# A linear-attention and adapter kernel: Q turned raw with relu on the way out of PSUM, sine taken from cosine by a tangent, all casts done by the loads, and a new written-out order

## The chip, the cores and the metric

The kernel runs on one core of a Trainium2 chip. The metric is device time in microseconds (us) of one execution. A core has engines that each work through their own instruction list in order: TensorE (PE in the profile, with PEld for its weight loads), VectorE (DVE), ScalarE (ACT), GpSimd (POOL) and SyncE (SP). [...] Transfers between HBM and the on-chip memory SBUF are issued by SyncE or GpSimd and carried by 16 DMA engines. TensorE writes to PSUM, from which VectorE and ScalarE move results to SBUF.

## The reference

Inputs are q, k and v of 8 batches, 8 heads, 576 positions and 64 features in float32, and small router weights. Cut to what matters:

```python
theta = pi/2 * pos / S                      # per position
phi(x) = concat([relu(x)*cos, relu(x)*sin]) # 128 features
kv  = einsum('bhsf,bhsd->bhfd', phi(k), v)
z   = phi(k).sum(over s)
x   = (phi(q) @ kv) / (phi(q) . z + 1e-6)   # attention output, (4608, 512)
logits = x @ w_gate                         # 8 experts
w = softmax of the two largest logits
out = x + sum over the two experts e of w_e * (x @ A[e]) @ B[e]   # rank 16
```

The output is 4608 by 512 in float32 (9.4 MB); q, k and v are 9.4 MB each.

## The kernel before, in words

**Tiling.** Positions are split as p*9 + j, with 64 values of p and 9 of j. The work goes in four pairs P of batches (2P and 2P+1). For each pair the kernel first builds the two feature matrices, then runs nine steps j of 128 rows (64 positions of each batch). Rows leave in units of three steps (the last pair has units of 3, 3, 2 and 1).

**Building a pair.** V arrives by GpSimd's loads, which cast float32 to bf16 (`ld_vh`, `ld_full`). `vscale` (L374) writes V times cos and V times sin into VV; since the weights depend on the position only, scaling V serves instead of scaling K. For pairs 1 to 3 the sine half is a GpSimd product of two tensors and the cosine half a VectorE product. K of the first pair comes as float32 by SyncE (`ld_f`) and ScalarE casts it with relu (L357); later K is cast by the load and gets relu on VectorE (L363). `kv_mm` (L388) multiplies K by VV on TensorE into pND, and `kv_evac` (L406, L408) copies it into BD, one half on ScalarE and one on VectorE. A column of cos and sin in VV yields z along with kv.

**Q.** All of q comes as float32 by SyncE into the eight F buffers. ScalarE casts it with relu into Qr (L368). In each step `qt_mm` (L469) turns Qr on TensorE, 128 columns at a time, into the PSUM tile pt, and `qt_evac` (L476) multiplies it by cos and by sin from the table TB in one VectorE product of 1024 elements, into qTcs.

**A step.** `num_mm` (L491) gives numerator and denominator in pND; VectorE takes the reciprocal (L504) and the product xt (L510). TensorE turns xt (L520) and ScalarE copies it (L526). For a unit, `za_mm` (L533) gives adapter inputs and logits in pza, VectorE and ScalarE do the two-expert softmax (`r_max`, `r_mask`, `r_sig`, L544 to L568), VectorE scales the adapter inputs (L571), TensorE turns them (L580), ScalarE copies (L585), `dx_mm` (L590, L591) adds x and the adapters' output in pdx, ScalarE copies to osb (L596) and SyncE stores (L602).

**What sets the order.** A planner in the file (`Planner.run`) lists all steps with their durations, due times, needs and buffers, plays them through once as the program is built, and emits the instructions in the order found, with a manual schedule. So each engine has one fixed list. Buffers come from pools of fixed size; a step that wants a buffer waits until its last user is done. PSUM has two pND tiles (two banks each), two pt, one pza and one pdx.

Of the kernel before, what the change touches and what calls it, by code (L numbers as in the profile page):

```python
# [19 lines left out]
LATENCY = {"PE": 0.25, "DVE": 0.12, "ACT": 0.15, "POOL": 0.2, "SP": 0.0}  # L20
DMA_GBPS = 0.400
DMA_LATENCY = 2.0
DMA_LANES = 8


class Step:
    __slots__ = ("eng", "dur", "emit", "needs", "makes", "uses", "due", "name",
                 "size", "preds", "start", "end", "seen", "idx")

    def __init__(self, eng, dur, emit, needs, makes, uses, due, name, size):  # L30
        self.eng, self.dur, self.emit = eng, dur, emit
        self.needs, self.makes, self.uses = needs, makes, uses
        self.due, self.name, self.size = due, name, size
        self.preds = []
        self.start = None


class Planner:
# [3 lines left out]
    def __init__(self):  # L42
        self.steps = []
        self.pools = {}
        self.slot = {}
        self.queue = {}
# [5 lines left out]
    def add(self, eng, dur, emit, due, needs=(), makes=(), uses=(), name="", size=0):  # L52
        s = Step(eng, dur, emit, list(needs), list(makes), list(uses), due, name, size)
        s.idx = len(self.steps)
        self.steps.append(s)
        return s

    def run(self):
# [5 lines left out]
        users = {}  # L64
        for s in self.steps:
            s.preds = [made[n] for n in s.needs]
            for u in s.uses:
                if u not in users and self.queue[u[0]] is not None:
                    self.queue[u[0]].append(u)
                users.setdefault(u, []).append(s)  # L70
        left = {u: len(v) for u, v in users.items()}
        free_at = {p: [0.0] * n for p, n in self.pools.items()}
        succ = [[] for _ in self.steps]
        npred = [0] * len(self.steps)
        for s in self.steps:
            for p in {id(p): p for p in s.preds}.values():
                succ[p.idx].append(s)
                npred[s.idx] += 1
        ready = {e: [] for e in LATENCY}
        for s in self.steps:  # L80
            if npred[s.idx] == 0:
                ready[s.eng].append(s)
        etime = {e: 0.0 for e in LATENCY}
        lanes = {"SP": [], "POOL": []}
        server = 0.0
        order = []
        while len(order) < len(self.steps):
            best = None
            for e, lst in ready.items():
                cands = []  # L90
                for s in lst:
# [4 lines left out]
                    for u in s.uses:  # L96
                        if u not in self.slot:
                            f = free_at[u[0]]
                            m = min(f)
                            fifo = self.queue[u[0]]  # L100
                            if m == math.inf or (fifo and fifo[0] != u):
                                ok = False
                                break
                            t = max(t, m)
# [8 lines left out]
                t, s = min((c for c in cands if c[0] <= m + 0.12), key=lambda c: (c[1].due, c[0]))  # L113
                if best is None or t < best[0]:
                    best = (t, s)
            if best is None:
                held = {u: self.slot[u] for u in self.slot if left[u]}
                raise RuntimeError(f"plan: no step can go: {[(s.name, s.makes[:1], [u for u in s.uses if u not in self.slot]) for v in ready.values() for s in v]} held {held}")
# [11 lines left out]
            s.seen = s.end + LATENCY[s.eng]  # L130
            if s.size:
                server = max(server, s.start + 0.6) + s.size / DMA_GBPS * 1e-6
                s.seen = server + DMA_LATENCY - 0.6
                lanes[s.eng].append(s.seen)
            etime[s.eng] = s.end
            for u in s.uses:
                left[u] -= 1
                if left[u] == 0:
                    free_at[u[0]][self.slot[u]] = max(x.seen for x in users[u])
# [13 lines left out]
def kernel(  # L153
# [23 lines left out]
    HALF_B = 128 * 2 * J * D * 4  # L177

# [3 lines left out]
    def sb(shape, dtype, name, n=None):  # L182
        if n is None:
# [4 lines left out]
    POOLS = {"F": 8, "V": 4, "K": 4, "Q": 4, "VV": 4, "BD": 4, "QT": 3, "XT": 12, "XTT": 6,  # L188
             "ZG": 2, "ZGT": 2, "OSB": 3, "M8": 2, "W": 2, "RD": 3,
             "pND": 2, "pT": 2, "pZA": 1, "pDX": 1}  # L190
# [9 lines left out]
    TBi = sb([128, J, NP], I32, "TBi")  # L200
    TB = sb([128, 2, J, NP], FP16, "TB")
# [6 lines left out]
    tF = sb([128, 2, J, D], FP32, "F", POOLS["F"])  # L208
    tV = sb([128, 4, J, D], BF16, "Vb", POOLS["V"])
    tK = sb([128, 4, J, D], BF16, "Kr", POOLS["K"])  # L210
    tQ = sb([128, 2, J, 2, D], BF16, "Qr", POOLS["Q"])
# [9 lines left out]
    tNA = sb([128, 3], FP32, "nasum", POOLS["M8"])  # L221
    tSG = sb([128, 3, E], FP32, "sig", POOLS["W"])
# [3 lines left out]
    pT = [psum.tile([128, 1024], BF16, name=f"pt{i}") for i in range(2)]  # L226
    pZA = psum.tile([128, 512], FP32, name="pza")
    pDX = psum.tile([128, 512], FP32, name="pdx")

    def S_(u):  # L230
        return pl.slot[u]

# [10 lines left out]
    def c_tbi():  # L243
        nc.gpsimd.iota(TBi, pattern=[[1, J], [J, NP]], base=0, channel_multiplier=0)

# [4 lines left out]
    def c_tb():  # L250
        nc.scalar.activation(TB[:, 1], TBi, AF.Sin, bias=0.0, scale=sc)
        nc.scalar.activation(TB[:, 0], TBi, AF.Sin, bias=halfpi[:, :], scale=-sc)

# [25 lines left out]
    pl.add("DVE", 0.1, c_halfpi, -50, makes=["halfpi"])  # L279
    pl.add("POOL", 0.5, c_tvi, -49.5, makes=["TVi"])  # L280
    pl.add("POOL", 0.9, c_tbi, -48.9, makes=["TBi"])
    pl.add("ACT", 2.0, c_tvf, -49, needs=["halfpi", "TVi"], makes=["TVf"])
    pl.add("ACT", 1.4, c_tb, -48, needs=["TBi", "TVf"], makes=["TB"])
    pl.add("ACT", 1.4, c_sig, -47, needs=["TB"], makes=["sigtab"])
    pl.add("DVE", 1.3, c_tv, -48, needs=["TVf"], makes=["TV"])
    for i in range(4):
        pl.add("DVE", 0.15, c_vcol(i), -47 + i, needs=["TVf"], makes=[("vcol", i)])
        pl.add("DVE", 0.4, c_bd(i), -40 + i, makes=[("bd", i)])
    pl.add("POOL", 1.0, c_ident, -47, makes=["ident"])
    pl.add("POOL", 3.0, c_s4, -20, needs=["ident"], makes=["S4"])  # L290
# [11 lines left out]
    pl.add("POOL", 0.9, w_a, -9, makes=["Ald"], size=1024 * 512)  # L302
    pl.add("POOL", 0.3, w_g, -9, makes=["Gld"], size=128 * 512)
    pl.add("POOL", 0.3, w_b, -8, makes=["Ball"], size=128 * 2048)

    def w_turn():
        for c in range(4):
            for i in range(4):
                nc.tensor.matmul(out=pDX[:, c * 128:(c + 1) * 128], lhsT=S4[:, i, c * 128:(c + 1) * 128],
                                 rhs=Ald[:, :, i, :], start=(i == 0), stop=(i == 3))  # L310
        for c in range(4):
            for i in range(4):
                nc.tensor.matmul(out=pZA[:, c * 8:(c + 1) * 8], lhsT=S4[:, i, c * 128:(c + 1) * 128],
                                 rhs=Gld[:, i, :], start=(i == 0), stop=(i == 3))

    def w_aw():
        nc.scalar.copy(AW[:, :, 0:ER], pDX.rearrange("p (c x) -> p c x", c=4))
        nc.scalar.copy(AW[:, :, ER:AW_W], pZA[:, 0:32].rearrange("p (c x) -> p c x", c=4))

    pl.add("PE", 2.0, w_turn, 2, needs=["S4", "Ald", "Gld"], makes=["AWp"],  # L320
           uses=[("pDX", "w"), ("pZA", "w")])
    pl.add("ACT", 0.8, w_aw, 3, needs=["AWp"], makes=["AW"], uses=[("pDX", "w"), ("pZA", "w")])


    T = 2.35
# [14 lines left out]
    def ld_f(x, b, a, u):  # L340
        def f():
            nc.sync.dma_start(out=flat(tF[S_(u)]), in_=half_src(x, b, a))
        return f

    def ld_vh(b, a, u):
        def f():
            nc.gpsimd.dma_start(out=flat(tV[S_(u)])[:, 2 * a:2 * a + 2], in_=half_src(v, b, a))  # L347
        return f

    def ld_full(x, b, u, ts):  # L350
        def f():
            nc.gpsimd.dma_start(out=flat(ts[S_(u)]), in_=full_src(x, b))
        return f

    def relu_k_half(b, a, uf, uk):
        def f():
            nc.scalar.activation(tK[S_(uk)][:, 2 * a:2 * a + 2], tF[S_(uf)], AF.Relu)  # L357
        return f

    def relu_k_full(uk):  # L360
        def f():
            t = tK[S_(uk)].rearrange("p c j d -> p (c j d)")
            nc.vector.tensor_scalar(out=t, in0=t, scalar1=0.0, scalar2=None, op0=ALU.max)  # L363
        return f

    def relu_q(b, a, uf, uq):
        def f():
            nc.scalar.activation(tQ[S_(uq)][:, a].rearrange("p j h d -> p h j d"), tF[S_(uf)], AF.Relu)  # L368
        return f

    def vscale(eng, cs, lo, hi, uv, uvv):
        def f():
            n = hi - lo
            eng.tensor_tensor(  # L374
                out=tVV[S_(uvv)][:, lo:hi, :, cs * (D + 2):cs * (D + 2) + D],
                in0=tV[S_(uv)][:, lo:hi],
                in1=TV[:, cs].unsqueeze(1).to_broadcast([128, n, J, D]),
                op=ALU.mult)
# [18 lines left out]
    def kv_evac(par, aa, up, ubd, eng):  # L397
        def f():
            pt, bd = pND[S_(up)], tBD[S_(ubd)]
            lo, n = aa[0], len(aa)  # L400
            for hh in range(2):
                o = bd[64 * hh:64 * hh + 64, par, lo:lo + n, :, 66 * hh:66 * hh + W]
                i = pt[64 * hh:64 * hh + 64, par, lo * 2 * W:(lo + n) * 2 * W].rearrange(
                    "p (a c w) -> p a c w", a=n, c=2)
                if eng == "ACT":
                    nc.scalar.copy(o, i)  # L406
                else:
                    nc.vector.tensor_copy(o, i)  # L408
        return f

    for P in range(4):
        for a in range(2):
            for b2 in range(2):
                b = 2 * P + b2
                uk, uv, uvv, ubd, uq = ("K", b), ("V", b), ("VV", b), ("BD", b), ("Q", b)
                uf = ("F", "q", b, a)
# [283 lines left out]
```

## Time and profile before

| | |
|---|---|
| median time of 2 runs | 161.36 us (161.11 to 161.61) |
| span of the profiled execution | 159.0 us |
| granted TensorE clock, mean | 0.915 |
| HBM read, written | 28.85 MB, 9.44 MB |

The profile shows, for one execution, how long each engine was busy, in groups of instructions by line, engine and shapes. A row of a group gives the busy time and the mean time of one instruction in ns, then how long the engine had been idle before such instructions and what ended the wait. The timeline lists instructions by start and length. A wait is put down to what released it last. The chain of waits is the path followed back from the last instruction.

### The profile page before, as it was taken

The page shows a single profiled execution, that of the slowest core. Times are in us where ns is not written, and L with a number is a line of the kernel's source. Part 1 is how long each engine was busy: PE and PEld are TensorE (multiplying, and loading weights), DVE is VectorE, ACT ScalarE, POOL GpSimd, SP SyncE. Part 2 cuts the span into 40 slices and gives each one's busy share as a digit, 9 for nine tenths or more (in the row PEclk, how much of TensorE's full clock was granted, in tenths as well). Part 3 has the DMA queues.
Part 4 walks back from the last instruction along what each step waited for, and adds up shares of the span by engine and source line. Part 5 has one row for each costly group of instructions (what it writes and reads, how often), then busy time and mean ns, then how long its engine had stood idle before and what let it go on. Part 6 is the DMA issues. An engine that isn't in the chain of part 4 may idle for free.

```text
span 159.0 us, 4155 instructions
## 1 busy us (share of the span) xinstructions
PE 101.1 (64%) x1724; PEld 73.4 (46%) x1724; DVE 110.8 (70%) x273; ACT 84.2 (53%) x170; POOL 49.4 (31%) x39
## 2 busy tenths in 40 slices
PE   0014365237976977206957986889988888797650
PEld 0013244125954546103846864656656565465310
DVE  5335284886268466998999698987876787869510
ACT  4922943301666433800862467985686546664751
POOL 6995106813239206999950000000000000000000
PEclk9999999999998589955796599999999999999996
DMA  4999999999999999999910004004422440315044
GB/s 164 309 288 292 292 293 286 327 339 307 288 279 275 287 244 293 220 208 207 277 66 0 4 0 198 4 6 198 194 108 103 196 198 6 148 49 202 0 198 198
DMA packets 16081, 30.01 MB, mean 189 GB/s; under 512 B 1984, under 2 KB 9280, under 8 KB 16064
## 3 DMA queue, kind: packets, MB, share of 16 engines
q1 hardware_dynamic: 7312, 21.24, 36.2%
q0 software_dynamic: 8752, 8.53, 32.1%
q8 instruction: 13, 0.21, 0.5%
q14 instruction: 4, 0.03, 0.1%
HBM read 28.85 MB, written 9.44 MB: 241 GB/s over the span
## 4 chain that ended last, share of the span: by engine, by line
DVE 30%; PE 27%; DMA 21%; POOL 7%; ACT 7%; issue 5%; ACTq 0%; POOLq 0%
DMA Vb<-in_v_dram 21%; DVE VV L374 9%; PE pnd L491 6%; DVE xt L510 6%; DVE qTcs L476 5%; PE pdx L590 5%; PE pdx L591 4%; PE pnd L388 4%; PE pza L533 3%; DVE BD L408 3%; ACT osb L596 3%; DVE Kr L363 2%; PE pt L520 2%; POOL Vb L347 2%; DVE rden L504 2%
## 5 line engine op out<-in xcount | busy, mean ns | idle before, releaser
L491 PE MATMUL pnd<-BD,qTcs 128*64 128x130 bf16 x576 | 27.9, 243 | 17.6 <-DVE xt L510 8.3
L491 PEld LDWEIGHTS <-qTcs 128*64 128x64 bf16 x576 | 20.7, 120 | 25.4 <-issue 12.9
L374 POOL TENSOR_TENSOR VV<-Vb,TV 128x2304 bf16<-128x2304 bf16 x6 | 29.9, 4989 | 4.4 <-DMA Vb<-in_v_dram 4.2
L596 ACT COPY osb<-pdx 128x512 f32<-128x512 f32 x36 | 21.2, 588 | 16.4 <-PE pdx L591 16.2
L526 ACT COPY xT<-pt 128x512 bf16<-128x512 bf16 x36 | 21.1, 594 | 15.9 <-PE pt L520 15.7
L374 DVE TENSOR_TENSOR VV<-Vb,TV 128x1152 bf16<-128x1152 bf16 (+1 forms) x14 | 24.7, 1786 | 6.8 <-DMA Vb<-in_v_dram 6.7
L476 DVE TENSOR_TENSOR qTcs<-pt,TB 128x1024 bf16<-128x1024 bf16 (+1 forms) x45 | 25.0, 576 | 3.9 <-PE pt L469 3.6
L510 DVE TENSOR_TENSOR xt<-pnd,rden 128x512 bf16<-128x512 f32 (+1 forms) x45 | 26.3, 584 | 1.3
L388 PE MATMUL pnd<-VV,Kr 64*64 64x130 bf16 x576 | 14.1, 264 | 17.9 <-DVE VV L374 14.7
L368 ACT ACTIVATE Qr<-F 128x1152 bf16<-128x1152 f32 x16 | 18.5, 1169 | 6.2 <-DMA F<-in_q_dram 6.2
L388 PEld LDWEIGHTS <-Kr 64*64 64x64 bf16 x576 | 12.4, 135 | 19.3 <-issue 10.0
L469 PE MATMUL pt<-ident,Qr 128*128 128x128 bf16 x144 | 16.0, 242 | 7.4 <-ACT Qr L368 3.4
L590 PE MATMUL pdx<-xt,ident 128*128 128x512 bf16 x36 | 14.7, 408 | 4.0 <-ACT osb L596 3.9
L520 PE MATMUL pt<-ident,xt 128*128 128x128 bf16 x144 | 14.9, 232 | 3.1 <-DVE qTcs L476 1.1
L406 ACT CAST BD<-pnd 64x260 bf16<-64x260 f32 (+1 forms) x20 | 6.6, 332 | 18.7 <-PE pnd L388 12.7
L469 PEld LDWEIGHTS <-Qr 128*128 128x128 bf16 x144 | 10.5, 107 | 12.3 <-issue 5.6
L504 DVE RECIPROCAL rden<-pnd 128x8 f32<-128x8 f32 (+1 forms) x45 | 8.7, 192 | 10.5 <-PE pnd L491 10.4
L591 PE MATMUL pdx<-Ball,zgT 128*128 128x512 bf16 x36 | 14.5, 404 | 0.9 <-ACT zgT L585 0.8
L408 DVE CAST BD<-pnd 64x260 bf16<-64x260 f32 (+1 forms) x20 | 7.5, 374 | 9.4 <-ACT BD L406 7.2
L520 PEld LDWEIGHTS <-xt 128*128 128x128 bf16 x144 | 10.6, 103 | 7.4 <-issue 2.8
L533 PE MATMUL pza<-AW,xT 128*128 128x136 bf16 x144 | 12.2, 239 | 0.2 <-ACT xT L526 0.2
L561 ACT ACTIVATE sig<-pza,nasum 128x8 f32<-128x8 f32 x36 | 7.1, 269 | 8.0 <-DVE pza L551 8.0
(46 smaller groups left out, 92.2 us busy)
## 6 DMA issues: line engine op xcount, KB each, us to landing
F<-in_q_dram SPq DMA_DIRECT2D x16, 576.0 KB, 16.8
out_dram<-osb SPq DMA_DIRECT2D x11, 768.0 KB, 3.3
Vb<-in_v_dram POOLq DMA_DIRECT2D x6, 576.0 KB, 32.0
Kr<-in_k_dram POOLq DMA_DIRECT2D x6, 576.0 KB, 29.9
F<-in_k_dram SPq DMA_DIRECT2D x4, 576.0 KB, 9.0
Vb<-in_v_dram POOLq DMA_DIRECT2D x4, 288.0 KB, 10.5
out_dram<-osb SPq DMA_DIRECT2D x1, 512.0 KB, 2.6
out_dram<-osb SPq DMA_DIRECT2D x1, 256.0 KB, 2.0
```

What stands on the lines that cost most here:

```text
L368: nc.scalar.activation(tQ[S_(uq)][:, a].rearrange("p j h d -> p h j d"), tF[S_(uf)], AF.Relu)
L374: eng.tensor_tensor(out=tVV[S_(uvv)][:, lo:hi, :, cs * (D + 2):cs * (D + 2) + D], in0=tV[S_(uv)][:, lo:hi], in1=TV[:, cs].unsqueeze(1).to_ ...
L388: nc.tensor.matmul(out=pt[64 * hh:64 * hh + 64, par, a * 2 * W:(a + 1) * 2 * W], lhsT=kt[64 * par:64 * par + 64, 2 * a + hh, j, :], rhs=vt ...
L469: nc.tensor.transpose(out=pt[:, o:o + 128], in_=qt[:, a, j].rearrange("p h d -> p (h d)"), identity=ident)
L476: nc.vector.tensor_tensor(out=tQT[S_(uqt)][:, :, 0:n, :], in0=pT[S_(up)][:, 0:n * 64].rearrange("p (g s) -> p g s", g=n).unsqueeze(1).to_b ...
L491: nc.tensor.matmul(out=nd[64 * b2:64 * b2 + 64, a, 0:4 * W].rearrange("p (h e w) -> p h e w", h=2, e=2)[:, :, par], lhsT=qt[:, cs, (b2 * l ...
L510: nc.vector.tensor_tensor(out=tXT[S_(uxt)].rearrange("p (a h d) -> p a h d", a=2, h=4)[:, aa[0]:aa[-1] + 1], in0=nd_view(und, aa)[:, :, :, ...
L520: nc.tensor.transpose(out=pT[S_(up)][:, c * 128:(c + 1) * 128], in_=tXT[S_(uxt)][:, c * 128:(c + 1) * 128], identity=ident)
L526: nc.scalar.copy(tXTT[S_(uxtt)].rearrange("p c s -> p (c s)"), pT[S_(up)][:, 0:512])
L590: nc.tensor.matmul(out=pDX, lhsT=ident, rhs=tXT[S_(uxt)], start=True, stop=False)
L591: nc.tensor.matmul(out=pDX, lhsT=tZGT[S_(uzt)][:, i], rhs=Ball, start=False, stop=True)
L596: nc.scalar.copy(tOSB[S_(uo)][:, i], pDX)
```

## The change

It moves the casts, the relu and part of the scaling to other places, and writes the order anew.

- **Loads.** K, V and Q all come by GpSimd's casting loads straight to bf16 (`load`); the F buffers and ScalarE's cast of Q go, and SyncE issues stores only. The first pair comes in halves. K gets its relu in place, on VectorE, ScalarE or GpSimd (`relu_k`).
- **Q.** Raw Q is turned in 64-column pieces (two per former piece). ScalarE applies relu as it copies from PSUM, which gives relu(q) without the cosine. VectorE writes a second copy times tan. The cosine of the query row cancels between numerator and denominator, so cos and sin become 1 and tan. The tan table is built by two TensorE matmuls in place of two sine passes.
- **V.** GpSimd no longer runs a product of two tensors; where it scales V, it does so in nine one-input instructions with a per-partition scalar. ScalarE can do the same in nine activations, VectorE by the product with TV as before.
- **Router.** One sigmoid per unit, preceded by a small VectorE operation, in place of one per step.
- **PSUM.** pt, pza and pdx become one pool of four banks, ps. The evacuation of K times V is cut by heads instead of parity. qTcs has ten buffers instead of three, Q six instead of four.
- **Tail.** In the last pair's last two units the two matmuls of dx are separate steps, and osb is copied in two halves, one on each engine.
- **Order.** Each step has a due time from a table (PLACES), and, where there are alternatives, its engine from another (CHOICE). Of the twelve whole and eight half V products VectorE then has eight and five, ScalarE three and three, GpSimd one whole; ten of the xT, five of the zgT and six whole and two half osb copies go to VectorE.

```diff
+PLACES = [
...
+]
+CHOICE = [
...
+]
...
+        if PLACES is not None:
+            for s in self.steps:
+                s.due = PLACES[s.idx]
+                s.choose(CHOICE[s.idx])
...
-    POOLS = {"F": 8, "V": 4, "K": 4, "Q": 4, "VV": 4, "BD": 4, "QT": 3, "XT": 12, "XTT": 6,
+    POOLS = {"V": 4, "K": 4, "Q": 6, "VV": 4, "BD": 4, "QT": 10, "XT": 12, "XTT": 6,
              "ZG": 2, "ZGT": 2, "OSB": 3, "M8": 2, "W": 2, "RD": 3,
-             "pND": 2, "pT": 2, "pZA": 1, "pDX": 1}
+             "pND": 2, "pS": 4}
...
+    def c_tan_p():
+        nc.vector.memset(ones_f, 1.0)
+        nc.vector.reciprocal(tan_p, TVf[:, 0])
+        nc.vector.tensor_tensor(out=tan_p, in0=tan_p, in1=TVf[:, 1], op=ALU.mult)
...
+    def c_tan_mm():
+        d = tan_d.rearrange("p j s -> p (j s)")
+        nc.tensor.matmul(out=pF(("pS", "t0")), lhsT=ones_f, rhs=d[:, 0:512], start=True, stop=True)
+        nc.tensor.matmul(out=pF(("pS", "t1"))[:, 0:64], lhsT=ones_f, rhs=d[:, 512:576], start=True, stop=True)
...
-    def ld_f(x, b, a, u):
-        def f():
-            nc.sync.dma_start(out=flat(tF[S_(u)]), in_=half_src(x, b, a))
-        return f
...
-    def relu_q(b, a, uf, uq):
-        def f():
-            nc.scalar.activation(tQ[S_(uq)][:, a].rearrange("p j h d -> p h j d"), tF[S_(uf)], AF.Relu)
-        return f
...
+    def load(x, b, hs, ts, u):
+        def f():
+            if len(hs) == 4:
+                nc.gpsimd.dma_start(out=flat(ts[S_(u)]), in_=full_src(x, b))
...
+    def relu_k(eng, hs, uk):
+        def f():
+            t = tK[S_(uk)][:, hs[0]:hs[-1] + 1].rearrange("p c j d -> p (c j d)")
+            if eng == "ACT":
+                nc.scalar.activation(t, t, AF.Relu)
+            else:
+                (nc.gpsimd if eng == "POOL" else nc.vector).tensor_scalar(out=t, in0=t, scalar1=0.0, scalar2=None, op0=ALU.max)
...
+            if eng == "POOL":
+                for j in range(J):
+                    nc.gpsimd.tensor_scalar(out=o[:, :, j], in0=i[:, :, j], scalar1=TVf[:, cs, j:j + 1],
+                                            scalar2=None, op0=ALU.mult)
+            elif eng == "ACT":
+                for j in range(J):
+                    nc.scalar.activation(o[:, :, j], i[:, :, j], AF.Copy, scale=TVf[:, cs, j:j + 1])
...
     def qt_mm(P, j, aa, up):
...
-                    nc.tensor.transpose(out=pt[:, o:o + 128], in_=qt[:, a, j].rearrange("p h d -> p (h d)"),
-                                        identity=ident)
+                    for hh in range(2):
+                        nc.tensor.transpose(out=pt[64 * hh:64 * hh + 64, o:o + 128], in_=qt[:, 2 * a + hh, j, :],
+                                            identity=ident)
...
+    def qt_evac(aa, up, uqt):
+        def f():
+            n = 4 * len(aa)
+            nc.scalar.activation(tQT[S_(uqt)][:, 0, 0:n].rearrange("p g s -> p (g s)"), pB(up)[:, 0:n * 64], AF.Relu)
+        return f
+
+    def qt_tan(j, aa, uqt):
+        def f():
+            n = 4 * len(aa)
+            t = tQT[S_(uqt)]
+            nc.vector.tensor_tensor(out=t[:, 1, 0:n], in0=t[:, 0, 0:n],
+                                    in1=TT[:, j].unsqueeze(1).to_broadcast([128, n, NP]), op=ALU.mult)
+        return f
...
+            nc.vector.scalar_tensor_tensor(
+                out=tTT[S_(um)][:, 0:n], in0=lg, scalar=2.0,
+                in1=tNA[S_(um)][:, 0:n].unsqueeze(2).to_broadcast([128, n, E]), op0=ALU.mult, op1=ALU.add)
...
-            for i in range(n):
-                nc.scalar.activation(tSG[S_(uw)][:, i], za_v(n)[:, i, ER:AW_W], AF.Sigmoid,
-                                     bias=tNA[S_(um)][:, i:i + 1], scale=2.0)
+            nc.scalar.activation(tSG[S_(uw)][:, 0:n], tTT[S_(um)][:, 0:n], AF.Sigmoid)
```

## The prediction

> **What bounds the kernel now.** I read the page from the top: totals, then the slices, then the busy time of three stretches, then the chain and the timeline of the worst stretch.
>
> ```profile
> span 159.0 us, 4155 instructions
> PE 101.1 (64%) x1724; PEld 73.4 (46%) x1724; DVE 110.8 (70%) x273; ACT 84.2 (53%) x170; POOL 49.4 (31%) x39
> ...
> POOL 6995106813239206999950000000000000000000
> PEclk9999999999998589955796599999999999999996
> DMA  4999999999999999999910004004422440315044
> ```
>
> No engine is full over the span. A slice is 3.98 us: the DMA engines are full until about 80 us, then nearly idle. So the first half waits for loads and the second for computing. The stretches (columns: length, then busy us of PE, PEld, DVE, ACT, POOL, then the clock, DMA share and GB/s) say so in numbers:
>
> ```profile
> 0.00:46.00 46.00, 20.07 (x380) 15.90 (x380) 25.09 (x61) 20.37 (x32) 22.53 (x32) 1.00 1.08 290
> 46.00:82.00 36.00, 22.73 (x382) 15.99 (x380) 30.09 (x55) 17.81 (x33) 26.87 (x7) 0.76 1.11 241
> 82.00:152.00 70.00, 56.70 (x961) 41.09 (x961) 55.59 (x158) 44.05 (x104) 0.00 (x0) 0.95 0.23 92
> ```
>
> By 46 us TensorE has done 20 of its 101 us. In the last stretch PE is busy 81% and VectorE 79%; within it, from 100 to 120 us, PE reaches 18.11 of 20 us.
>
> The chain of waits in order of time, and the timeline from 60 to 84 us (start, length), name the two early losses:
>
> ```profile
> 13.36 32.82 DMA Vb<-in_v_dram
> ```
>
> ```profile
> 63.22 8.97 DVE L374 TENSOR_TENSOR VV<-Vb,TV 128x2304 bf16<-128x2304 bf16 x1
> 75.67 1.55 DVE L363 TENSOR_SCALAR Kr<-Kr 128x2304 bf16<-128x2304 bf16 x1
> 79.72 3.13 DVE L374 TENSOR_TENSOR VV<-Vb,TV 128x2304 bf16<-128x2304 bf16 x1
> 73.09 1.09 PE L491 MATMUL pnd<-BD,qTcs 128*64 128x130 bf16 x16 [7.99 <-DVE xt L510]
> 61.93 19.71 POOL L374 TENSOR_TENSOR VV<-Vb,TV 128x2304 bf16<-128x2304 bf16 x4
> ```
>
> First, a V tile issued at 13.4 us lands at 46.2, because q for all pairs was queued at the same time on SyncE. Second, four GpSimd products stand back to back from 61.9 to 81.6 us; beside them one VectorE product lasts 8.97 us, where the same shape takes 1.35 us at 93.75 us. PE idles 8 us behind it. Excess of these three VectorE rows over 1.35, 0.75 and 1.35: 10.2 us.
>
> **What the Trainium skill says.** "SBUF — State Buffer", Who interferes with whom: a VectorE instruction with two SBUF inputs contends with a GpSimd instruction that reads SBUF, and whichever issues first holds the pair for its whole length. The 8.97 us agree. By that wording a one-input GpSimd instruction that reads SBUF still contends; no row here shows one. "DMA: Bandwidth & Descriptors", Issuing engines are not separate DMA queues: all queues share 16 engines, so moving q to GpSimd's queue adds no bandwidth in itself. "VectorE: DVE Perf Modes", The perf-mode tier table: a 16-bit tensor_tensor in SBUF runs at 2x, one with a PSUM operand at 1x. Here the PSUM one (qTcs) makes 1024 elements in 0.683 us, so it isn't at half the rate of VV (1.35 us for 2304); I use the rows. "TensorEngine Tiling (Array Packing)", Key Properties: different tiles run in parallel. L491 agrees: 16 matmuls of 130 columns on 64-column tiles take 0.66 us.
>
> **The change, part by part.** The prices are these rows (busy us, mean ns):
>
> ```profile
> L596 ACT COPY osb<-pdx 128x512 f32<-128x512 f32 x36 | 21.2, 588 | 16.4 <-PE pdx L591 16.2
> L526 ACT COPY xT<-pt 128x512 bf16<-128x512 bf16 x36 | 21.1, 594 | 15.9 <-PE pt L520 15.7
> L368 ACT ACTIVATE Qr<-F 128x1152 bf16<-128x1152 f32 x16 | 18.5, 1169 | 6.2 <-DMA F<-in_q_dram 6.2
> L476 DVE TENSOR_TENSOR qTcs<-pt,TB 128x1024 bf16<-128x1024 bf16 (+1 forms) x45 | 25.0, 576 | 3.9 <-PE pt L469 3.6
> ```
>
> *Loads.* With GpSimd's queue alone, from 66 to 76 us:
>
> ```profile
> DMA packets 1863, 2.08 MB, mean 208 GB/s; under 512 B 60, under 2 KB 1863, under 8 KB 1863
> ...
> q0 software_dynamic: 1863, 2.08, 121.4%
> ```
>
> It writes 208 GB/s of bf16. K, V and Q are 14.15 MB in bf16 and the weights 0.27: 69 us. They now go in order of need: the first pair's twelve halves (3.54 MB, 17 us) are in at about 21 us, the second pair's six loads and the weights (3.81 MB, 18 us) at about 39. Before, its last V came at 46.2. Stores (0.79 MB, landing 3.3 us after issue by the page) take about 2 us each from the loads, so the last load lands at 75 to 82 us, as before; only the last quarter of the work needs it. 30 loads and three weights stand in one in-order queue with GpSimd's computing. Behind its one VV product are the loads of the fourth pair; up to seven earlier ones (about 20 us of transfers) cover that, so I cost it at nothing.
>
> *VectorE.* From 110.8: qTcs -25.0. The tan product is not in the trace; its price comes from VV, 0.745 us for 1152 elements (the shortest) and 1.35 for 2304, that is 0.14 + 0.000525 per element: 0.41 for 512 and 0.28 for 256, so 27 x 0.41 + 18 x 0.28 = +16.0 (at the rate of L510, 0.69 and 0.42, it would be 26.3; the two-input form in SBUF makes me take the lower). The GpSimd lock -10.2. VV: eight full and five half products for six and eight: +0.5. K relu: three full and two halves for six full: -1.4. Evacuations moved from ScalarE: ten xT at 0.42 and five zgT at 0.36 (qTcs's 512 form), six osb at 0.69 and two halves at 0.42 (xt's rows): +11.0. Fewer BD copies: -2.5. A small product before each sigmoid, 12 x 0.18: +2.2. Constants +1.3. Sum 102.7. Three GpSimd instruction groups still read SBUF (one VV in nine pieces, two relus of a whole K); a GpSimd product took 4.5 us alone, one can hold a tan product for none to all of that, and I take 4 us in all (0 to 12). VectorE: about 107 (103 to 120).
>
> *ScalarE.* From 84.2: Qr -18.5; sin tables -1.4; 36 sigmoids to 12, -3.7; relu out of PSUM 27 x 0.594 + 18 x 0.378 = +22.8; V scaled in 54 small activations with a scale pointer (0.269 us for 8 elements, and about 0.82 ns for each further one, less overlap) +20; moved to VectorE -12.3; the rest 0. About 91.
>
> *TensorE.* Each Q transpose of 128 columns becomes two of 64. Four take 0.22 us at 109.66; eight, priced by L491, 8 x 0.04 = 0.31: 36 x 0.09 = +3. The tan broadcast +1 to 2. 101.1 becomes 105, or less where the clock (0.76 from 46 to 82 us) stays up.
>
> *Buffers.* Four shared PSUM banks instead of two pT, one pZA and one pDX, and ten qTcs instead of three, aim at the waits 16.2 (osb on PE) and 15.7 (xT on PE). A wait is added: PE's product now waits for ScalarE, then VectorE, not VectorE alone, and pND stands behind it. The ten qTcs let both run ahead, so it is hidden except where a pair's first Q arrives.
>
> *Sum.* VectorE (107) and TensorE (105) bound together. In the first 10 us only 5 of VectorE's 107 can be done, and after its last product about 4 us pass (7 before, from 152 to 159; the last evacuation is now halved). The 102 between run at a share of 0.87: above the 0.79 of 82 to 152 us, below the 0.905 that PE reached from 100 to 120. 102 / 0.87 = 117; 10 + 117 + 4 = 131 us.
>
> **The rivals.** (a) The chain of small waits keeps the pace, as before: share 0.79 and a tail of 5 to 7, 10 + 129 + 6 = 145. For it: three engines are now near 90 to 107 and each row goes through all of them; against: the deeper buffers. (b) The order fits so well that the bound runs at 0.93: 10 + 110 + 4 = 124; for it 100 to 120 us in the trace, against it the wait for the second pair's data near 39 us. (c) The single load queue stalls behind GpSimd's relus or blocked slots: the fourth pair's nine steps take at least 9 x 2.8 = 25 us (25 steps took 70 us before) plus 4, so to end at 165 its Q would have to land near 136, 54 us late; only nested waits would do that, and GpSimd's waits of 9.1 and 8.1 us before show that such waits exist. That ends slower.
>
> **How the numbers follow.** Forecast (126 to 137) 0.50; (a) 137 to 150, 0.27; (b) 115 to 126, 0.18; (c) 0.03; between, 0.02. The range 119 to 144 leaves out the far ends of (a) and (b), about 0.2. Faster by over 2% (under 158): 0.96; same 0.01; slower 0.03.
>
> **What would show it.** Loads on one queue near 208 GB/s, the second pair complete near 39 us; no VectorE product over about 5 us; the tan product near 0.41; VectorE's total 103 to 110, ScalarE near 91; VectorE busy over 85% from 40 to 120 us. Wrong if tan runs near 0.69, if GpSimd's relu or VV blocks VectorE for over 10 us in all, or if PE waits for ScalarE's relu in every step.

## The result, and the profile after

The kernel after takes 131.9 us (131.68 to 132.12), against 161.36 before: a ratio of 0.817, interval 0.809 to 0.825. The forecast was 131, in a range of 119 to 144. Some executions of a kernel come out over 1.5% above its fastest; the medians here and below are over all of them, the ratios leave those out.

The page of the kernel after, its totals and slices (3.25 us each):

```profile
span 129.9 us, 4453 instructions
PE 96.9 (75%) x1860; PEld 72.9 (56%) x1872; DVE 107.3 (83%) x300; ACT 88.4 (68%) x200; POOL 51.4 (40%) x57
...
POOL 6999963216629998499100059300000000000000
...
DMA  1999999999999999999999999900000656005583
GB/s 10 178 178 202 206 207 206 207 192 207 209 207 208 211 357 292 207 209 208 206 225 313 205 256 278 288 32 8 0 5 8 271 214 238 9 32 216 242 351 136
```

TensorE's work is about the same as before; it is packed closer. The DMA engines are still full until about 82 us, but at 207 GB/s of bf16 on one queue. Adding up the GB/s slices gives 7.2 MB by 39 us; by this count the first two pairs and the weights (7.35 MB) are in at about 40.

The stretches (columns as in the prediction):

```profile
0.00:46.00 46.00, 31.06 (x589) 23.90 (x592) 35.77 (x110) 33.78 (x87) 31.41 (x47) 0.93 1.15 190
46.00:82.00 36.00, 28.02 (x619) 21.57 (x617) 31.49 (x63) 26.10 (x52) 19.59 (x11) 0.91 1.17 248
```

By 46 us TensorE has been busy for 31.1 us (20.1 before), by 82 us for 59.1 (42.8 before). Two thirds of this lead is thus made in the first 46 us.

The groups that the prediction priced (busy us, mean ns, idle before):

```profile
L593 DVE TENSOR_TENSOR xt<-pnd,rden 128x512 bf16<-128x512 f32 (+1 forms) x45 | 25.8, 581 | 1.1
L555 ACT ACTIVATE qTcs<-ps 128x512 bf16<-128x512 bf16 (+1 forms) x45 | 21.3, 512 | 4.8 <-PE ps L548 4.5
L609 ACT COPY xT<-ps 128x512 bf16<-128x512 bf16 x26 | 15.2, 585 | 12.3 <-PE ps L603 12.3
L562 DVE TENSOR_TENSOR qTcs<-qTcs,TT 128x512 bf16<-128x512 bf16 (+1 forms) x45 | 19.6, 457 | 0.4 <-ACT qTcs L555 0.2
L609 ACT COPY osb<-ps 128x512 f32<-128x512 f32 (+1 forms) x31 | 16.5, 561 | 3.3 <-PE ps L683 1.6
L448 POOL TENSOR_SCALAR Kr<-Kr 128x2304 bf16<-128x2304 bf16 x2 | 12.1, 6056 | 15.7 <-DMA Kr<-in_k_dram 15.7
```

ScalarE's wait ahead of osb fell from 16.4 to 3.3 us; ahead of xT it fell only from 15.9 to 12.3, though ten of 36 copies are now on VectorE. VectorE hardly waits for its tan product (0.4 us in all). The last row is new: GpSimd's relu of one K takes 6 us. The timeline around both of them (start, length) shows what that does to VectorE:

```profile
54.48 6.03 POOL L448 TENSOR_SCALAR Kr<-Kr 128x2304 bf16<-128x2304 bf16 x1 [1.45 <-DMA Kr<-in_k_dram]
55.81 4.88 DVE L562 TENSOR_TENSOR qTcs<-qTcs,TT 128x512 bf16<-128x512 bf16 x2
60.75 0.60 PE L574 MATMUL pnd<-BD,qTcs 128*64 128x130 bf16 x14 [2.42 <-DVE qTcs L562]
76.30 6.08 POOL L448 TENSOR_SCALAR Kr<-Kr 128x2304 bf16<-128x2304 bf16 x1 [14.27 <-DMA Kr<-in_k_dram]
77.34 5.66 DVE L448 TENSOR_SCALAR Kr<-Kr 128x2304 bf16<-128x2304 bf16 x1
83.64 0.61 PE L603 MATMUL ps<-ident,xt 128*128 128x128 bf16 x4 [3.60 <-DVE xt L593]
```

Two tan products take 4.88 us in place of 0.82; a VectorE relu takes 5.66 us in place of 0.75. That is 9.0 us of VectorE, in two pieces that each end within 0.7 us of the GpSimd instruction's end. The profile counts them as busy time, though VectorE does nothing more in them. TensorE stands 2.4 us behind the first and 3.6 behind the second. "SBUF — State Buffer", Who interferes with whom, of the Trainium skill says it so: VectorE's tensor_scalar in a two-port mode, and a product with two SBUF inputs, can be shut out by a GpSimd instruction that reads SBUF for its whole length. A product and a relu are both held here; that the relu ran in a two-port mode, no run shows.

### The profile page after: what moved, and what is told of

Read it like the earlier page. It is cut to its first block, busy times and chain, and to the rows that moved or that the text cites. A ratio compares the mean times of both kernels' runs of the same rounds, so it can differ in the third digit from the quotient of the medians.

```text
span 129.9 us, 4453 instructions
## 1 busy us (share of the span) xinstructions
PE 96.9 (75%) x1860; PEld 72.9 (56%) x1872; DVE 107.3 (83%) x300; ACT 88.4 (68%) x200; POOL 51.4 (40%) x57
## 3 DMA queue, kind: packets, MB, share of 16 engines
q1 hardware_dynamic: 1872, 9.44, 18.1%
## 4 chain that ended last, share of the span: by engine, by line
PE 35%; DVE 28%; ACT 10%; POOL 10%; issue 8%; DMA 5%; POOLq 0%; DVEq 0%; ACTq 0%
PE pnd L574 10%; PE pnd L474 7%; POOL VV L458 7%; DVE xt L593 6%; PE ps L622 5%; DMA Kr<-in_k_dram 5%; DVE qTcs L562 5%; ACT VV L462 5%; PE ps L548 4%; PE ps L603 4%; DVE Kr L448 3%; DVE VV L464 3%; PE ps L681 3%; DVE zg L661 2%; PE ps L683 2%
## 5 line engine op out<-in xcount | busy, mean ns | idle before, releaser
L555 ACT ACTIVATE qTcs<-ps 128x512 bf16<-128x512 bf16 (+1 forms) x45 | 21.3, 512 | 4.8 <-PE ps L548 4.5
L609 ACT COPY xT<-ps 128x512 bf16<-128x512 bf16 x26 | 15.2, 585 | 12.3 <-PE ps L603 12.3
L462 ACT ACTIVATE VV<-Vb,TVf 128x128 bf16<-128x128 bf16 (+1 forms) x54 | 19.3, 443 | 2.6 <-DMA Vb<-in_v_dram 2.6
L562 DVE TENSOR_TENSOR qTcs<-qTcs,TT 128x512 bf16<-128x512 bf16 (+1 forms) x45 | 19.6, 457 | 0.4 <-ACT qTcs L555 0.2
L609 ACT COPY osb<-ps 128x512 f32<-128x512 f32 (+1 forms) x31 | 16.5, 561 | 3.3 <-PE ps L683 1.6
L603 PE MATMUL ps<-ident,xt 128*128 128x128 bf16 x144 | 14.2, 229 | 5.8 <-DVE xt L593 5.5
L448 POOL TENSOR_SCALAR Kr<-Kr 128x2304 bf16<-128x2304 bf16 x2 | 12.1, 6056 | 15.7 <-DMA Kr<-in_k_dram 15.7
L464 DVE TENSOR_TENSOR VV<-Vb,TV 128x2304 bf16<-128x2304 bf16 (+1 forms) x13 | 14.5, 1130 | 1.3 <-DMA Vb<-in_v_dram 1.3
L548 PE MATMUL ps<-ident,Qb 128*64 128x128 bf16 x288 | 15.0, 248 | 0.1
L681 PE MATMUL ps<-xt,ident 128*128 128x512 bf16 x34 | 13.0, 381 | 0.6 <-DVE osb L611 0.3
## 6 DMA issues: line engine op xcount, KB each, us to landing
Kr<-in_k_dram POOLq DMA_DIRECT2D x6, 576.0 KB, 20.1
```

What stands on the lines that cost most here:

```text
L448: (nc.gpsimd if eng == "POOL" else nc.vector).tensor_scalar(out=t, in0=t, scalar1=0.0, scalar2=None, op0=ALU.max)
L462: nc.scalar.activation(o[:, :, j], i[:, :, j], AF.Copy, scale=TVf[:, cs, j:j + 1])
L548: nc.tensor.transpose(out=pt[64 * hh:64 * hh + 64, o:o + 128], in_=qt[:, 2 * a + hh, j, :], identity=ident)
L555: nc.scalar.activation(tQT[S_(uqt)][:, 0, 0:n].rearrange("p g s -> p (g s)"), pB(up)[:, 0:n * 64], AF.Relu)
L562: nc.vector.tensor_tensor(out=t[:, 1, 0:n], in0=t[:, 0, 0:n], in1=TT[:, j].unsqueeze(1).to_broadcast([128, n, NP]), op=ALU.mult)
L603: nc.tensor.transpose(out=pB(up)[:, c * 128:(c + 1) * 128], in_=tXT[S_(uxt)][:, c * 128:(c + 1) * 128], identity=ident)
```

## The experiments

The runs were made in several sets, each beside the kernel before. Differences between kernels are taken from the ratios to the kernel before, times 161 us.

| kernel | median us | ratio to before | interval |
|---|---|---|---|
| after | 131.9 | 0.817 | 0.809 to 0.825 |
| K relu off GpSimd | 125.9 | 0.781 | 0.774 to 0.788 |
| V product off GpSimd | 132.5 | 0.824 | 0.819 to 0.829 |
| no GpSimd arithmetic | 126.5 | 0.785 | 0.778 to 0.791 |
| tan left out | 129.6 | 0.800 | 0.792 to 0.808 |
| Q's relu on VectorE | 135.9 | 0.842 | 0.827 to 0.858 |
| planner's plain order | 130.7 | 0.816 | 0.806 to 0.827 |
| plain order, old buffers | 133.2 | 0.829 | 0.822 to 0.835 |
| no GpSimd, no tan | 125.3 | 0.780 | 0.776 to 0.785 |
| no GpSimd, x not added | 124.3 | 0.766 | 0.758 to 0.774 |
| before, V product off GpSimd | 157.9 | 0.977 | 0.958 to 0.997 |
| before, q after k and v | 167.7 | 1.047 | 1.033 to 1.061 |
| before, one load queue | 146.0 | 0.911 | 0.904 to 0.917 |

### What GpSimd's arithmetic costs

Three kernels keep the written-out order and put GpSimd's steps, in their places, on VectorE: the two relus, the V product, or both.

```diff
-                                ("POOL", 3.0 * len(aa), relu_k("POOL", hs, uk))], d + 3,
+                                ("POOL", 3.0 * len(aa), relu_k("DVE", hs, uk))], d + 3,
...
-                            ("POOL", 4.7 if half else 7.6, vscale("POOL", cs, hs, uv, uvv))]
+                            ("POOL", 4.7 if half else 7.6, vscale("DVE", cs, hs, uv, uvv))]
```

> The changed kernel, with GpSimd's two relus of a whole K (6.06 us each) given to VectorE at the same places of the order, 0.75 us each. My theory: VectorE is the bound and the two relus hold its shared port; the two long rows beside them (4.54 us for a tan product, 5.66 us for a K relu, against 0.42 and 0.75) vanish, VectorE's total falls from 107.3 to about 100, and the time by 5 to 9 us, to 123 to 127. Rival: the locks fall where VectorE would have waited anyway, and nothing moves beyond 1 us (131 to 133).

> The changed kernel, with GpSimd's one V product in nine pieces (10.07 us, 39.3 to 49.3 us) made by VectorE as one product of 1.35 us. My theory: TensorE's wait for it is only about 2 us and VectorE takes 1.35 us more, so 0 to 2 us are gained: 130 to 132. Rival: it delays the second pair as a whole (the chain of waits goes through it for 6.7% of the span), and 4 to 7 us are gained: 125 to 128.

> Both edits at once: GpSimd only issues loads after the constants. My theory: the sum of both, 7 to 10 us less than the changed kernel, 122 to 125, with no VectorE row over 1.6 us. Rival (the pace is set by the chain of small waits): under 3 us gained, 129 or more.

Without the two relus the time falls by 0.036 x 161 = 5.8 us. Moving the V product changes nothing that can be told, and both together give 5.2 us: as the relus alone, and less than the 7 to 10 expected. So putting relus on GpSimd was a mistake of this change, worth 5 to 6 us, and the V product cost nothing although it lasts 10 us:

```profile
39.26 10.07 POOL L458 TENSOR_SCALAR VV<-Vb,TVf 128x256 bf16<-128x256 bf16 x9 [1.54 <-DVE zgT L611]
```

That one is nine instructions of 1.1 us. Beside it the longest VectorE product of V took 1.55 us instead of 1.35. That VectorE gets in between short pieces is the reading of this; no run splits the relu into pieces.

The two relus did not cost the same. TensorE has the same list in these kernels, so the number of weight loads (PEld) that it has done tells where it stands. In the kernel after and in the one without GpSimd arithmetic it has done 1032 and 1035 of them at 70 us, and 1182 and 1184 at 78 us; then 1209 and 1247 at 84, and 1253 and 1383 at 90. So the first relu cost nothing in the end, and the whole loss comes with the second. The K of the first relu lands at 54.4 us, so the relu has to wait for it on either engine. On VectorE it holds up VectorE's list: at 56 us TensorE is then behind (734 weight loads, against 785 in the kernel after). After the second relu TensorE is 4 us late (1233 weight loads at 86 us instead of 82), and about 5 us late by 92. From 84 to 92 us the granted clock is 0.50, against 0.79 without GpSimd arithmetic; how much of the loss is the clock's is not separated. No wait of TensorE is put down to a GpSimd relu itself, so it is VectorE's delay that reaches TensorE, not a late K.

### Is VectorE the bound?

The tan product is left out (the cosine half is used twice), once in the kernel after and once with no GpSimd arithmetic:

```diff
-            nc.vector.tensor_tensor(out=t[:, 1, 0:n], in0=t[:, 0, 0:n],
-                                    in1=TT[:, j].unsqueeze(1).to_broadcast([128, n, NP]), op=ALU.mult)
+            return
...
-                                lhsT=qt[:, cs, (b2 * len(aa) + n) * 2 + par, :],
+                                lhsT=qt[:, 0, (b2 * len(aa) + n) * 2 + par, :],
```

> The changed kernel without the 45 tan products (left out: the sine half of the query; the product then uses the cosine half twice). My theory, VectorE is the bound: 19.6 us less work there, TensorE (97) and ScalarE (88) come next, so 8 to 14 us are gained: 118 to 124. Rival, the chain of small waits or TensorE is the bound: at most 4 us, 128 or more.

> Left out: the product with tan (the cosine half of Q is used in both products), 19.6 us of VectorE in the kernel after, and no GpSimd arithmetic, so that no GpSimd op holds VectorE. To be compared with the kernel without GpSimd arithmetic, 126.5 us. First theory, the one of the prediction: VectorE sets the pace; its total falls from 100.3 to about 83, so the time falls to 115 or less. Second theory: the pace is set by the arrival of each pair's loads up to about 60 us and by TensorE (94 us of work, 97% busy once the data is there); then 122 to 126, as with the GpSimd arithmetic left in (129.55 against 131.9).

VectorE's total falls by 13.1 us (107.3 to 94.2) in the first and 11.9 (100.3 to 88.4) in the second; the time falls by 0.018 x 161 = 2.8 us, and by nothing that the intervals can tell. So the theory of the prediction fails in both, and VectorE alone isn't the bound.

The totals fall by less than the tan products last (19.6 us in the first, 15.3 in the second), since neighbours on VectorE overlap in the timeline:

```profile
76.09 0.42 DVE L562 TENSOR_TENSOR qTcs<-qTcs,TT 128x512 bf16<-128x512 bf16 x1
76.43 0.27 DVE L587 RECIPROCAL rden<-pnd 128x8 f32<-128x8 f32 x2
```

The second starts 0.08 us before the first ends. For 45 products that makes 3.6 us, an estimate from this pair; it is the gap between 15.3 and 11.9. The opposite load, Q's relu from PSUM moved to VectorE:

```diff
-            nc.scalar.activation(tQT[S_(uqt)][:, 0, 0:n].rearrange("p g s -> p (g s)"), pB(up)[:, 0:n * 64], AF.Relu)
+            nc.vector.tensor_scalar(out=tQT[S_(uqt)][:, 0, 0:n].rearrange("p g s -> p (g s)"), in0=pB(up)[:, 0:n * 64], scalar1=0.0, scalar2=None, op0=ALU.max)
```

> The changed kernel, with the relu of Q out of PSUM on VectorE instead of ScalarE, at the same places of the order: VectorE makes two instructions where it made one (0.42 and 0.41 us for 512 elements). My theory, VectorE is the bound: 27 x 0.42 + 18 x 0.28 = 16 us more there, the time rises by 12 to 18 us, to 144 to 150. Rival (the hop from ScalarE to VectorE is what costs): VectorE's extra work is paid back by the missing hop, and the time rises by under 5 us.

VectorE grew by 11 us, to 118.3, and the time by 0.025 x 161 = 4 us, with a wide interval (0.827 to 0.858). About a third of the added work shows, as the rival had it, not all of it.

### Is TensorE the bound?

In the kernel without GpSimd arithmetic, the matmul that adds x is left out:

```diff
-            if part != 1:
-                nc.tensor.matmul(out=pF(udx), lhsT=ident, rhs=tXT[S_(uxt)], start=True, stop=False)
             if part != 0:
-                nc.tensor.matmul(out=pF(udx), lhsT=tZGT[S_(uzt)][:, i], rhs=Ball, start=False, stop=True)
+                nc.tensor.matmul(out=pF(udx), lhsT=tZGT[S_(uzt)][:, i], rhs=Ball, start=True, stop=True)
```

> Left out: the matmul with the identity that adds x to the experts' output in PSUM (36 of 128x128 by 128x512, about 0.22 to 0.25 us each, 8 to 9 us of TensorE); the output lacks x. No GpSimd arithmetic. To be compared with 126.5 us. Second theory (loads, then TensorE): two thirds of the 36 matmuls stand after the loads' end, so the time falls by 5 to 8 us, to 118 to 122. First theory (VectorE sets the pace): TensorE has the room, 125 to 127.

TensorE's busy time falls by 4.5 us (94.1 to 89.6), not 8 to 9, and the time by 2 (medians) to 3 us (ratios): between the two theories' figures. Set side by side, the stretches from 0 to 60 us and from 60 to 110 us in the kernels with no GpSimd arithmetic, with no tan, and with x not added, in this order:

```profile
0.00:60.00 60.00, 38.71 (x811) 29.42 (x812) 46.88 (x132) 43.57 (x105) 28.93 (x46) 0.94 1.15 205
60.00:110.00 50.00, 46.43 (x972) 34.91 (x972) 44.50 (x137) 37.65 (x79) 0.00 (x0) 0.97 0.69 173
```

```profile
0.00:60.00 60.00, 40.13 (x815) 31.12 (x815) 41.38 (x109) 43.71 (x106) 28.76 (x46) 0.89 1.15 205
60.00:110.00 50.00, 46.91 (x988) 35.39 (x986) 39.05 (x117) 38.43 (x81) 0.00 (x0) 0.97 0.69 173
```

```profile
0.00:60.00 60.00, 39.13 (x820) 30.15 (x822) 46.98 (x132) 44.40 (x107) 28.70 (x46) 0.92 1.15 205
60.00:110.00 50.00, 45.46 (x980) 34.50 (x976) 46.59 (x147) 38.65 (x81) 0.00 (x0) 0.96 0.72 184
```

Up to 60 us no engine is full: TensorE has been busy for 39 to 40 us in all three, and the one thing that is alike and full is the load stream at 205 GB/s. From 60 us on, TensorE is at 93% and VectorE at 89%. Without tan, VectorE drops to 78% and TensorE stays at 94%. With x not added, VectorE rises to 93% and TensorE falls to 91%.

The span from 60 us to the end (totals less the work up to 60 us) tells more. Without tan, VectorE has 6.4 us less to do there and the span ends 1.0 us sooner, about the noise. With x not added, TensorE has 4.9 us less to do there and the span ends 2.7 us sooner. So after 60 us TensorE is the nearer bound, with VectorE close behind it: about half of what is taken from TensorE shows, and next to nothing of what is taken from VectorE. In the kernel after, the same later stretch has only 42.75 us of TensorE, and GpSimd's second relu lies in it.

The chain of waits of the kernel with neither GpSimd arithmetic nor tan says the same of the first 60 us (start, length):

```profile
15.26 13.41 DMA Vb<-in_v_dram
...
30.70 23.54 DMA Kr<-in_k_dram
54.34 0.76 DVE Kr L448
```

Two loads make 37 of its first 54 us. In the kernel after, the page's chain runs through GpSimd's V product instead (7%). But moving that product gained nothing, and TensorE stands at the same weight load at 70 us with and without GpSimd arithmetic; a VectorE instruction held by GpSimd counts as work in the chain, and what GpSimd itself waited for, here the load of K, is not followed. That the loads set this part is read from the chains and from these counts; no run of this kernel made them faster.

### What the written-out order and the buffers are worth

First the tables are left out, so that the planner takes its own due times and the first-named engine of each step (no GpSimd arithmetic). Then, on top of this, the banks and the three qTcs of the kernel before, and no halving in the last units:

```diff
+PLACES = None
...
-    POOLS = {"V": 4, "K": 4, "Q": 6, "VV": 4, "BD": 4, "QT": 10, "XT": 12, "XTT": 6,
+    POOLS = {"V": 4, "K": 4, "Q": 6, "VV": 4, "BD": 4, "QT": 3, "XT": 12, "XTT": 6,
...
-             "pND": 2, "pS": 4}
+             "pND": 2, "pT": 2, "pZA": 1, "pDX": 1}
...
-                last = P == 3 and ui >= 2
+                last = False
```

> The changed kernel without the two tables: due times by the rule in each step, and each step on its first-named engine, so that all V products and K relus are VectorE's (9 us more than now) and all evacuations ScalarE's (11 us less for VectorE), with no GpSimd computing. My theory: the engines' totals stay near 100, and the order itself is worth a few per cent: 133 to 142. Rival: the order is worth nothing beside the missing locks, and it ends at 124 to 130.

> The kernel after in the planner's plain order with no GpSimd arithmetic (130.66 us), now with the PSUM banks of the kernel before: two for the transposes, one for the gate's product, one for the experts' output, where after has one pool of four for all; 3 buffers of turned Q in place of 10; and the last two groups not split in halves. Theory that the shared PSUM pool and the buffers carry the higher pace after the loads' end (TensorE 97% busy against 81% before): 137 to 143. Rival, that the order and the loads carry it and the buffers were never the limit: 129 to 133.

Against the kernel without GpSimd arithmetic, the plain order costs 0.0315 x 161 = 5.1 us, between the figures of its theory and its rival. That is the worth of the tables with nothing of GpSimd in them; the tables as they stand put the relus on GpSimd and lose it again: after and the plain order can't be told apart. The old buffers cost 0.0125 x 161 = 2.0 us more, and the intervals overlap. The theory that the shared banks and the ten qTcs carry the pace (137 to 143) is wrong.

### What of the change helps the kernel before

The kernel before, with its six GpSimd products of V on VectorE:

```diff
-                        pl.add("POOL", 5.2, vscale(nc.gpsimd, 1, 0, 4, uv, uvv), d,
+                        pl.add("DVE", 1.35, vscale(nc.vector, 1, 0, 4, uv, uvv), d + 2,
```

> The kernel before, with GpSimd's six V products (29.9 us) given to VectorE at 1.35 us each, planned anew. My theory: VectorE gains 10.2 us of locks and loses 8.1 of new work, but the stall of 8 us on TensorE and the loads stuck behind GpSimd go: 150 to 156. Rival: the loads bound the first half anyway, and nothing moves: 159 to 162.

This gives 0.023 x 161 = 3.6 us, with an interval from 0.5 to 6.8 us, so its size is unclear. Then, alone on the kernel before, q of the later pairs is placed in the plan behind the k and v of its batch:

```diff
-                pl.add("SP", 0.5, ld_f(q, b, a, uf), dq - (0 if P == 0 else 14), makes=[("ldq", b, a)], uses=[uf], size=HALF_B, name="ldq")
+                pl.add("SP", 0.5, ld_f(q, b, a, uf), dq - (0 if P == 0 else 14),
+                       needs=[] if P == 0 else [("ldk", b), ("ldv", b)], makes=[("ldq", b, a)], uses=[uf], size=HALF_B, name="ldq")
```

> The kernel before, with q of the pairs 1 to 3 loaded only when K and V of the same batch are in. My theory: the second pair's V lands near 36 us instead of 46, and 3 to 8 us are gained: 153 to 158. Rival: the bytes are the same and GpSimd's products set the pace after 46 us, so nothing is gained: 159 to 163.

It was slower, by 3 to 6%, where both theories had it at 163 us or less. But it doesn't test the order of loads: on SyncE's in-order list six of the eight q loads of the last two pairs came to stand behind stores and were issued only from 72 us on, and in the profiled run, at 174.9 us the longest of the four, one VectorE product met GpSimd's for 13.3 us. The better form puts all loads into GpSimd's casting queue, with V already off GpSimd:

```diff
-    tF = sb([128, 2, J, D], FP32, "F", POOLS["F"])
+    tF = sb([128, 2, J, D], BF16, "F", POOLS["F"])
...
-            nc.sync.dma_start(out=flat(tF[S_(u)]), in_=half_src(x, b, a))
+            nc.gpsimd.dma_start(out=flat(tF[S_(u)]), in_=half_src(x, b, a))
...
-                    pl.add("SP", 0.5, ld_f(k, b, a, ufk), d, makes=[("ldk", b, a)], uses=[ufk], size=HALF_B, name="ldk")
+                    pl.add("POOL", 0.5, ld_f(k, b, a, ufk), d, makes=[("ldk", b, a)], uses=[ufk], size=HALF_B, name="ldk")
...
-                pl.add("SP", 0.5, ld_f(q, b, a, uf), dq - (0 if P == 0 else 14), makes=[("ldq", b, a)], uses=[uf], size=HALF_B, name="ldq")
+                pl.add("POOL", 0.5, ld_f(q, b, a, uf), dq - (0 if P == 0 else 14), makes=[("ldq", b, a)], uses=[uf], size=HALF_B, name="ldq")
```

> The kernel before with its six V products of GpSimd on VectorE (157.85 us), and now Q of all pairs and K of the first pair also loaded by GpSimd's casting queue, in bf16, in the planner's order (each pair's V and K ahead of its Q), so that all loads stand in one queue; relu of Q stays on ScalarE ahead of the transposes. Theory that about 10 us of the gain come from the order of the loads in one queue (second pair's V at 46 us before, 39 us after): 146 to 150. Rival, that the loads' order is not the limit in the kernel before: 155 to 160.

The step is 0.067 x 161 = 10.8 us, give or take some 3 us by the two intervals, and the largest of any single run here (the planner lays out the order anew for it). The second pair's second product of K and V shows where it comes from; timelines of TensorE in the kernel before and with one queue:

```profile
59.62 1.24 PE L388 MATMUL pnd<-VV,Kr 64*64 64x130 bf16 x72 [0.28 <-DVE Kr L363]
```

```profile
38.80 1.25 PE L388 MATMUL pnd<-VV,Kr 64*64 64x130 bf16 x72 [0.77 <-DVE xt L510]
```

The second pair is ready for TensorE 21 us sooner, with the same bytes read from HBM; with V off GpSimd alone it stood at 60.9, so GpSimd's product wasn't what held it. The edit does two things that go together here, order and bf16 in one queue, and no run separates them. But the loads as a whole end no sooner. On the kernel before they end at about 79 us, and with one queue at about 83 (slices of 3.61 us):

```profile
DMA  2999999999999999999999910233105320532064
```

So a faster stream is not the cause. That leaves what lands first, with the order that the planner then lays out.

### The gain, step by step

From before to after, in us: V off GpSimd -3.6, one load queue -10.8, then (to the plain order with old buffers) 0.082 x 161 = -13.2, new buffers -2.0, tables -5.1, and +5.2 for what the tables put back on GpSimd. The step of 13.2 holds raw Q, relu out of PSUM, tan, the router's single sigmoid, the evacuation of K times V by heads, six Q buffers, the planner's new durations and due times, and the rest of the rewriting; the runs don't divide it, and each step is uncertain by 1.5 to 3 us. One part of it is visible: ScalarE's relu of Q ahead of the turn, 18.5 us in 16 instructions in the one-queue kernel, is gone, so Q can be turned as it lands; what that alone is worth was not tried.

## Why the prediction was right, and where it wasn't

- **The sum.** From 10 us to the end of VectorE's last instruction at 125.7, VectorE does 107.3 - 5.8 = 101.5 us of work in 115.7 us, a share of 0.877, with a tail of 4.2. The forecast had 102 at 0.87 and 4. It compared a sum that is a span (129.9) with a time (131.9), a slip of 2 us. That the parts of the sum came out so close is in part luck, as the next points and the one on VectorE's total show.
- **"VectorE (107) and TensorE (105) bound together"** is not what the runs show. Up to about 60 us the loads set the pace. After it, without GpSimd arithmetic, TensorE is the nearer bound and VectorE stands close behind. A single share of 0.87 over 117 us fitted as the mean of two parts with different limits. It would have been a bad guide to edits: by the forecast's sum, 13.1 us less of VectorE is worth 13.1 / 0.87 = 15 us, and it brought 2.8; 11.9 us less brought nothing that can be told.
- **Loads.** 208 GB/s, second pair in at 39, last load at 75 to 82 us: measured 207, about 40 and about 83. One queue, worth 10.8 us in the kernel before, was no term of the forecast's sum; there it stands only as a better fill.
- **The V product on GpSimd at nothing**: right, by the run that moves it.
- **The lock at 4 us (0 to 12)** was mis-sized: 9.0 us of VectorE, 5.8 us of time, all of it behind the second relu. The step took the old two-input GpSimd product's 4.5 us as the length; the one-input relu lasts 6.06, and both began just before a VectorE instruction, 1.0 to 1.3 us ahead of it, and held it to their end. The sign given for it, no product over about 5 us, was met and yet misleading: the longest wait sat in a relu (5.66), not a product.
- **The tan product at 0.41 and 0.28**: measured 0.41 where undisturbed and 0.284; the 19.6 us include 4.1 of the lock, so 15.5 against 16.0 (and 12 in the total, by the overlap).
- **VectorE 107**: 107.3, with 5 us more of the lock and 4.4 less elsewhere: two errors that cancel, which is luck. **ScalarE 91**: 88.4; relu out of PSUM 21.3 (22.8 expected), V in small activations 19.3 (20).
- **TensorE 105** was too high: 96.9 on the page, where 12 of 1872 matmuls are missing, and 94.1 to 96.5 in the three kernels with GpSimd's steps moved, where all are on record. The turn of Q, +3 expected, took 15.0 us in 288 pieces, where the 144 wide ones took 16.0. That two 64-column pieces run side by side fits this, and was not tested alone.
- **Buffers.** The 16.2 and 15.7 us that they aimed at are ScalarE's waits for TensorE. The wait ahead of osb fell to 3.3 us. In the plain order the old buffers put some of it back (3.1 us to 9.5) and cost only 2.0 us of time, within the noise: so this idle time of ScalarE was worth little.
- **VectorE over 85% busy from 40 to 120 us**: 72.3 of 80 us, 90%. As the experiments say, that is not proof of a bound.
- **Rival (b)**, 124 us at a share of 0.93: without the two relus the time comes near it, 125.9 us, but not in its way. Without any GpSimd arithmetic VectorE's share from 10 us to its last instruction at 120.4 is 94.5 / 110.4 = 0.86; the lock's 9 us are gone from its work, and the share is as before.

The best version seen that computes all of the reference is the kernel after with the K relus on VectorE, 125.9 us; without any GpSimd arithmetic it can't be told from this.

## What to carry to other kernels

When a load-bound start precedes a compute-bound end, look first at what lands first: all loads in one queue, in order of need, were worth about 11 us here with the same bytes read, though they ended no sooner. An engine at 90% busy is not yet the bound; leave out one of its operations and see whether the time follows. Keep long GpSimd instructions that read SBUF away from a VectorE that TensorE is waiting for: of two such instructions of 6 us one cost nothing and the other about 5 us, and 10 us in nine pieces cost nothing. Whether cutting a long one into pieces saves its cost was not tried. Where two kernels have the same list for an engine, count its instructions done by the same time: that shows where the time is lost.

## What was not expected of the hardware

- GpSimd's relu of 128x2304 bf16, one input, in place: 6.06 us, eight times VectorE's 0.75, and longer than its two-input product of the same size took alone before (4.55).
- VectorE's relu in place, with one SBUF input, was held by a GpSimd instruction (5.66 us) as a product with two inputs was (4.54).
- 288 turns of 64 columns took less time than 144 of 128: 15.0 against 16.0 us, and 14.3 against 15.8 between two kernels with the same mean granted clock (no GpSimd arithmetic, and one load queue on the kernel before).
- The mean granted clock did not go with the time in the two runs of the kernel after: 0.896 with 131.68 us, 0.931 with 132.12.
